# The products of p and V as four 32-column tiles of the TensorE array

## The chip, the cores and the metric

The kernel runs on one core of one Trainium2 chip. The metric is device time in microseconds (us); lower is better. Times of single instructions are in nanoseconds (ns). PE is TensorE's matmul, PEld its weight load, ACT is ScalarE, DVE is VectorE, POOL is GpSimd, SP is SyncE, which issues most DMAs. L1172 is line 1172 of the kernel before.

## What is computed

Three results are put together: a recurrent attention with memory over 64 segments of 32 tokens, a gated feed-forward block over all 2048 tokens, and a gate that mixes the two. All inputs are bf16; the width is 640, there are 32 heads of 192, the memory has 8 rows.

```python
for s in range(n_seg):                       # 64 segments, one after the other
    h = concatenate([mem, x[:, 32*s:32*s+32]], axis=1)      # 8 + 32 rows
    q, k, v = (einsum('btd,dhe->bhte', h, W) for W in (Wq, Wk, Wv))
    scores = where(mask, einsum('bhqe,bhke->bhqk', q, k) * scale, -1e9)
    p = softmax(scores, axis=-1)
    o = einsum('bhqk,bhke->bhqe', p, v)      # the product of p and V
    o = einsum('bhte,hed->btd', o, Wo)
    mem = o[:, :8]                           # the next segment needs it
    outs.append(o[:, 8:])
a = concatenate(outs, axis=1)
b = (gelu(x @ w_gate) * (x @ w_up)) @ w_down
out = g * a + (1 - g) * b                    # g = sigmoid((x * gate_w).sum(-1))
```

The memory makes the segments a chain: segment s+1 can't begin before the first rows of segment s are there.

## The kernel before, in words

The feed-forward block comes first (`ffn_gu`, `ffn_down`, the first 190 us or so of the execution). Then come the 64 segments, in `segment`. Weights of the attention don't all fit in the on-chip memory: most pieces stay there, and 17 slots (14 of 384 KB for Wq, Wk and Wv, 3 of 480 KB for Wo) hold two pieces by turns and are loaded anew in each segment by SP (`load_piece`, L597), as soon as the matmuls that read the old piece are done.

The order of the work within a segment is written out by hand in the list `PROG` (L504). Its entries are: `g` (the projections of a group of Q, K, V, one of five slices of the contraction at a time, L1039, and L226 where the weights in the array are kept), `tq` and `tk` (transposes of Q and K rows on DVE, L1073), `sc` (scores, L1080 to L1093), `ex` (softmax on DVE and ACT), `pt` (p is transposed on TensorE, L1139 and L1144, and ACT copies it out of PSUM, L1157), `pv` (the product of p and V, `pv_oct`), `wo` (the output projection, L1201, in the last octet L1224), and `lf` and `vb` (projections for rows of later segments, L882 and L1012). A segment has four octets of 8 heads (4 pairs of heads); `pv` stands in the list once for each. The engines' queues are filled in this order, and each engine works its queue off in order. Semaphore waits are put in by `_Sched`: an operation waits for the last writer of what it reads and for the readers of what it writes. If a PE operation has several waits, some may be moved onto the last instructions of the operation before it.

TensorE can be split by columns. A matmul with `tile_position=(0, 32*j)` and 32 columns of weights uses a quarter of the array and writes the PSUM partitions 32j to 32j+31; four of those, for j = 0 to 3, are issued one after another and run side by side. The projections, the transposes of p and the output projection are all of that kind. The scores use two halves of the array (40 columns of weights at column 0 or 64).

In `pv_oct`, for one octet: V is in `v_sb` (128 partitions: the 32 rows of the segment for each of 4 pairs), the part of V for the 8 memory rows of 4 segments is in `vl_sb`, and the transposed p is in `PTm` and `PTl` (index i: first or second head of a pair). The output has 384 columns of V, in three chunks c of 128; in chunk c the columns 64i to 64i+63 belong to head i. `half(c, i)` makes two matmuls for the 64 columns: one against `PTm[:, i]`, 160 columns moving (L1172), and one against `PTl[:, i]`, 64 columns moving, which adds to some of those results (L1174). Each matmul brings a weight load of its own. They are issued in the order of c, first the two of L1172 and then the two of L1174. So an octet has 12 matmuls and 12 weight loads. In every fourth segment (s % 4 == 0) the first of these stand in an operation of their own, named PV, which doesn't wait for `vl_sb`; the rest (PVa) does. After that ACT (L1183), and in the last octet also DVE (L1188), copies the result out of PSUM, and `wo` uses it.

Of the kernel before, what the change touches and what calls it, by code (L numbers as in the profile page):

```python
# [231 lines left out]
def _build(nc, A_x, A_mem0, A_Wq, A_Wk, A_Wv, A_Wo, seg_len, w_gate, w_up, w_down,  # L232
# [34 lines left out]
    S_ = _Sched(nc)  # L267
# [27 lines left out]
    NVB, NUB = 2, 2  # L295
# [35 lines left out]
    ps = nc.alloc_psum_tensor("ps", [128, 8, 512], F32)  # L331
# [3 lines left out]
    o = wsA_base - wsB_total  # L335
# [6 lines left out]
    o = wsA_base  # L342
# [4 lines left out]
    o = ffn_base  # L347
# [10 lines left out]
    def sreg(o, nbytes, plo=0, phi=128):  # L358
        return Rg("sb", o, o + nbytes, plo, phi)
# [35 lines left out]
    r_v = [sreg(wsB_off["v"] + b * 768, 768) for b in range(NVB)]  # L395
# [8 lines left out]
    PTm = PT[:, 0:PTW].rearrange("p (i t r) -> p i t r", t=4, r=R)  # L404
    PTl = PT[:, PTW:PTW + 128].rearrange("p (i t r) -> p i t r", t=4, r=16)
    r_PT = sreg(wsB_off["PT"], 2 * (PTW + 128))
# [23 lines left out]
    o = ffn_base - sum(fp_sz.values())  # L430
# [48 lines left out]
    r_ps = [Rg("ps", b, b + 1) for b in range(8)]  # L479
# [45 lines left out]
    def octet(s, i):  # L525
        return i if s % 2 == 0 else NOCT - 1 - i
# [35 lines left out]
    o = 0  # L562
# [71 lines left out]
    def load_residents(cls, pick=lambda key: True):  # L634
        for key in first:
# [7 lines left out]
           reads=[r_ident], writes=[r_ident])  # L643
    def asel(ap, reg, pattern, base, cm, fill):
# [12 lines left out]
           reads=[r_elw], writes=[r_elw])  # L657
# [19 lines left out]
    for h in range(NH):  # L677
        for w_, sb_, rw_, nm in ((w_gate, wg_sb, r_wg, "wg"), (w_up, wu_sb, r_wu, "wu")):
            S_.add("sp", lambda e, h=h, w_=w_, sb_=sb_: e.dma_start(
                sb_[h], w_.rearrange("(p k) f -> p k f", p=128)[:, :, FH * h:FH * (h + 1)]),  # L680
                writes=[rw_[h]], dma_sem="%s%d" % (nm, h))
# [228 lines left out]
    for n, (g, o) in enumerate(units):  # L910
# [7 lines left out]
        if g == 0:  # L918
            S_.add("pool", lambda e, o=o, b=b: e.tensor_copy(out=stg[:, o], in_=lst[b][:, 0]), reads=[r_lst[b]], writes=[r_stg[o]],
                   name="stg s0 o%d" % o)  # L920
# [69 lines left out]
    def misc_bank(s, group=9):  # L990
        tick[0] += 1
        ok = [b for b in (0, 1, 2, 3) + ((LB,) if s % 4 in (1, 2) or s % 4 == 3 and group < 3 else ()) + ((OB,) if group < 2 else ()) if b not in bk_of.values() and b not in lb.values()]
        b = min(ok, key=lambda b: misc[b])
        misc[b] = tick[0]
        return b

    def apx(ap, dims):
        return bass.AP(ap.tensor, ap.offset, [list(ap.ap[0])] + [list(d) for d in dims])
# [161 lines left out]
    def pv_oct(s, o):  # L1160
        A = misc_bank(s)
        B = misc_bank(s) if o in USPLIT else A
        oc = octet(s, o)
        v, vl, u = v_sb[o % NVB], vl_sb[oc], uT[o % NUB]
        ru = r_uTp[o % NUB]
        W = 4 * R

        def half(c, i):
            full = ps[64 * i:64 * i + 64, B if c == 2 else A, W * c:W * c + W]
            part = full.rearrange("p (t r) -> p t r", r=R)[:, :, XA:R]  # L1170
            e0 = 128 * c + 64 * i
            return [lambda e: e.matmul(full, v[:, e0:e0 + 64], PTm[:, i], start=True, stop=False,  # L1172
                                       tile_position=(0, 64 * i), skip_group_check=True),
                    lambda e: e.matmul(part, vl[:, e0:e0 + 64], PTl[:, i], start=False, stop=True,  # L1174
                                       tile_position=(0, 64 * i), skip_group_check=True)]

        fns = [x for c in range(3) for y in zip(half(c, 0), half(c, 1)) for x in y]
        if s % 4 == 0:
            S_.add("pe", fns[:2], reads=[r_v[o % NVB], r_PT], writes=[r_ps[A]], name="PV s%d o%d" % (s, o))
            del fns[:2]  # L1180
        S_.add("pe", fns, reads=[r_v[o % NVB], r_vl[oc], r_PT], writes=[r_ps[A]] + ([r_ps[B]] if B != A else []), name="PVa s%d o%d" % (s, o))
        na = 2 if o in USPLIT else 3
        S_.add("act", lambda e: e.activation(  # L1183
            out=apx(u[:, 0, 0, :], [[R, na], [3 * R, 4], [1, R]]),
            in_=ps[:, A, 0:na * W].rearrange("p (c t r) -> p c t r", t=4, r=R), func=ACTF.Copy),
            reads=[r_ps[A]], writes=[ru[0]] if na == 2 else ru, name="uT evac s%d o%d" % (s, o))
        if na == 2:
            S_.add("dve", lambda e: e.tensor_copy(out=u[:, :, 2, :], in_=ps[:, B, 2 * W:3 * W].rearrange("p (t r) -> p t r", r=R)),  # L1188
                   reads=[r_ps[B]], writes=[ru[1]], name="uT mid s%d o%d" % (s, o))
        q = s % 4  # L1190
        S_.add("pool", lambda e: e.tensor_copy(  # L1191
            out=uTl[:, 12 * oc:12 * oc + 12, M * q:M * q + M].rearrange("p (t c) i -> p t c i", c=3), in_=u[:, :, :, L:R]),
            reads=[r_uT[o % NUB]], writes=[r_uTl[oc]], name="uTl s%d o%d" % (s, o))
# [71 lines left out]
    def segment(s):  # L1265
# [3 lines left out]
        for n, item in enumerate(PROG):  # L1269
# [25 lines left out]
            elif kind == "pt":  # L1295
                p_transp(s, i)
            elif kind == "pv":
                pv_oct(s, i)
            elif kind == "lf":
                if i == q and unit(s, item[2]):  # L1300
                    if item[3] == 0:
                        for m in range(2):
                            lb[item[2], m] = misc_bank(s)
                    for m in range(2):
                        LBK[m] = lb[item[2], m]
                    left_mm(*unit(s, item[2]), item[3], unit_piece)
            elif kind == "vb":
                if q == 3 and g + 1 < NG:
                    if i == 0:
                        lb["v"] = misc_bank(s)  # L1310
                    vl_mm(s + 1, i)
            elif kind == "le":
                if i == q and unit(s, item[2]):
                    if n > n_wo:
                        post.append(item[2:])
                    else:
                        left_evac(s, *item[2:])
            else:
                held = wo_part(s, item)
                if i == 2 and item[2] == 0 and q == 0 and g > 0:  # L1320
                    outl_store(g - 1)
                if q == 3 and item != items[-1]:
                    wo_left(s, held)
# [116 lines left out]
```

## Time and profile before

| | |
|---|---|
| Median of 3 runs | 1802.42 us (1795.88 to 1802.75) |
| Span of the profiled execution, first to last instruction | 1783.4 us |
| Mean granted TensorE clock | 0.998 |
| PE busy | 1629.5 us, 91% |
| Chain that ended last | PE 69%, DMA 13%, DVE 8%, ACT 6%, issue 4% |
| Data moved by DMA | 524.33 MB, 294 GB/s over the span |
| L1172: 1536 matmuls, mean of one | 243 ns |
| L1174: 1536 matmuls, mean of one | 194 ns |
| Weight loads of L1172 and L1174, mean of one | 109 and 112 ns |

The profile gives of the profiled execution its span; the runs' times also hold what lies around the span, and a time of the profiled execution with that is not shown. Busy time counts a time once in which several matmuls of an engine overlap, and a matmul's mean is its length from start to modelled end. "issue" stands for time in which an engine waited for nothing that the profile shows. A table of windows has, for each stretch, its length, the busy time of PE, PEld, DVE, ACT and POOL with the number of instructions in brackets, the granted clock, the DMA engines' share (by packets that start in the window, so it can pass 1) and GB/s.

### The profile page before, as it was taken

The numbers are of one execution on the slowest core, as the hardware profiler recorded it, in microseconds if no ns is written. First come the engines' busy times: TensorE is split into PE (matmuls) and PEld (weight loads), VectorE is DVE, ScalarE is ACT, GpSimd is POOL, SyncE is SP. The second block draws the span as 40 slices with busy tenths as digits, with TensorE's granted clock in tenths as the row PEclk, the third lists the DMA queues.
The fourth block names the chain that finished last, engine by engine and source line by source line (L and its number), as shares of the span: only waits on it lengthen the run. The fifth ranks groups of instructions, "written<-read, shape, count | busy, mean of one in ns | idle before, by whom it ended". The sixth has DMA issues, their size and how long they took to land.

```text
span 1783.4 us, 80070 instructions
## 1 busy us (share of the span) xinstructions
PE 1629.5 (91%) x39162; PEld 817.9 (46%) x31501; DVE 957.7 (54%) x2932; ACT 793.8 (45%) x1835; POOL 319.8 (18%) x1099
## 2 busy tenths in 40 slices
PE   9999989899998999899899999899999989899987
PEld 4554444454444444454444444454444444454443
DVE  2223555555555655555565655555555655555554
ACT  3222444444444444444444444444444544444443
POOL 1100111111211111111111111111211111111211
PEclk9999999999999999999999999999999999999999
DMA  9815887888788887888788887888888887888786
GB/s 332 297 45 177 329 318 266 324 322 316 289 295 298 318 311 261 318 318 315 287 299 299 311 319 263 322 310 319 298 299 300 317 290 269 321 313 321 289 303 260
DMA packets 263390, 524.33 MB, mean 294 GB/s; under 512 B 97384, under 2 KB 116224, under 8 KB 263040
## 3 DMA queue, kind: packets, MB, share of 16 engines
q1 hardware_dynamic: 259912, 516.11, 79.5%
q8 instruction: 276, 4.52, 1.0%
q10 hardware_dynamic: 3128, 3.09, 0.5%
q14 instruction: 74, 0.61, 0.1%
HBM read 498.00 MB, written 21.11 MB: 291 GB/s over the span
## 4 chain that ended last, share of the span: by engine, by line
PE 69%; DMA 13%; DVE 8%; ACT 6%; issue 4%; SPq 0%; DVEq 0%; ACTq 0%
PE ps L1039 20%; PE ps L226 15%; PE ps L1201 8%; DMA arena<-in_A_Wv_dram 7%; PE ps L1172 3%; DMA left_qk_scratch<-arena 3%; PE ps L802 3%; PE ps L799 3%; PE ps L882 3%; DVE arena L889 3%; PE ps L1093 2%; PE ps L817 2%; ACT arena L887 2%; PE ps L1080 2%; PE ps L1088 2%
## 5 line engine op out<-in xcount | busy, mean ns | idle before, releaser
L1039 PE MATMUL ps<-arena 128*32 128x384 bf16 x9940 | 734.8, 328 | 58.5 <-DVE arena L1344 40.4
L226 PE MATMUL ps<-arena 128*32 128x384 bf16 x7680 | 584.4, 326 | 10.8 <-ACT arena L887 6.1
L1039 PEld LDWEIGHTS ps<-arena 128*32 128x32 bf16 x9940 | 254.0, 96 | 420.1 <-issue 244.4
L1073 DVE STREAM_TRANSPOSE arena<-arena 128x384 bf16<-128x384 bf16 x512 | 279.0, 564 | 227.0 <-ACT arena L1059 226.6
L1059 ACT ACTIVATE arena<-ps 128x384 bf16<-128x384 f32 x512 | 236.2, 489 | 176.3 <-PE ps L1039 164.4
L1201 PE MATMUL ps<-arena 128*32 128x320 bf16 x6144 | 297.0, 300 | 16.1 <-issue 15.5
L1201 PEld LDWEIGHTS ps<-arena 128*32 128x32 bf16 x6144 | 163.6, 97 | 75.7 <-issue 26.5
L1119 ACT ACTIVATE ps<-ps 104x160 f32<-104x160 f32 x256 | 74.3, 290 | 236.4 <-DVE ps L1109 236.4
L1107 DVE TENSOR_REDUCE arena<-ps 104x4 f32<-104x160 f32 x256 | 83.1, 325 | 176.0 <-PE ps L1093 175.7
L1157 ACT ACTIVATE arena<-ps 128x448 bf16<-128x448 f32 x192 | 104.8, 546 | 143.3 <-PE ps L1144 143.3
L1191 POOL COPY arena<-arena 128x96 bf16<-128x96 bf16 x256 | 68.4, 267 | 522.6 <-ACT arena L1183 419.3
L936 POOL COPY arena<-arena 128x96 bf16<-128x96 bf16 x256 | 70.0, 274 | 498.7 <-PE ps L1093 436.3
L1183 ACT ACTIVATE arena<-ps 128x480 bf16<-128x480 f32 (+1 forms) x256 | 138.1, 540 | 34.0 <-PE ps L1174 29.0
L1062 ACT ACTIVATE arena<-ps 128x384 bf16<-128x384 f32 x256 | 124.8, 488 | 52.7 <-PE ps L1039 52.4
L1172 PE MATMUL ps<-arena 128*64 128x160 bf16 x1536 | 122.1, 243 | 10.4 <-issue 3.4
L1172 PEld LDWEIGHTS ps<-arena 128*64 128x64 bf16 x1536 | 80.6, 109 | 97.9 <-ACT arena L1157 46.6
L882 PE MATMUL ps<-arena 128*32 128x384 bf16 x1280 | 111.1, 330 | 1.2 <-issue 1.2
L1174 PE MATMUL ps<-arena 128*64 128x64 bf16 x1536 | 105.1, 194 | 5.8 <-issue 5.8
L1121 DVE TENSOR_REDUCE arena<-ps 104x4 f32<-104x160 f32 x256 | 81.8, 320 | 51.6 <-ACT ps L1119 43.9
L889 DVE STREAM_TRANSPOSE arena<-arena 128x384 bf16<-128x384 bf16 x128 | 73.8, 577 | 57.4 <-ACT arena L887 52.6
L1224 PE MATMUL ps<-arena 128*32 128x160 bf16 x3072 | 77.1, 234 | 22.2 <-DMA arena<-in_A_Wo_dram 12.6
L887 ACT ACTIVATE arena<-ps 128x384 bf16<-128x384 f32 x128 | 62.4, 490 | 67.6 <-DVE arena L889 38.5
(84 smaller groups left out, 1816.7 us busy)
## 6 DMA issues: line engine op xcount, KB each, us to landing
arena<-in_A_Wk_dram SPq DMA_DIRECT2D x335, 384.0 KB, 7.7
arena<-in_A_Wv_dram SPq DMA_DIRECT2D x335, 384.0 KB, 9.4
arena<-in_A_Wq_dram SPq DMA_DIRECT2D x272, 384.0 KB, 5.6
arena<-in_A_Wo_dram SPq DMA_DIRECT2D x205, 480.0 KB, 7.4
left_qk_scratch<-arena SPq DMA_DIRECT2D x64, 192.0 KB, 2.6
arena<-left_qk_scratch SPq DMA_DIRECT2D x63, 192.0 KB, 7.8
ffn_b_scratch<-arena ACTq DMA_DIRECT2D x16, 160.0 KB, 3.7
arena<-ffn_b_scratch SPq DMA_DIRECT2D x64, 40.0 KB
```

What stands on the lines that cost most here:

```text
L226: return e.add_instruction(mybir.InstMatmult(name=nm, start_tensor_calc=like["start"], stop_tensor_calc=stop, tile_size=(128, 32), tile_po ...
L882: fns.append(lambda e, outp=outp, rhs=rhs, j=j: e.matmul(outp, lhs, rhs, start=(k == 0), stop=(k == KT - 1), tile_position=(0, 32 * j)))
L889: S_.add("dve", lambda e: e.transpose(out=dst[:, :, m].rearrange("p q c i -> p c q i"), in_=rowl.rearrange("p (c r) -> p c r", r=L)), read ...
L1039: fns.append(lambda e, outp=outp, rhs=rhs, j=j: e.matmul(outp, lhs, rhs, start=(k == 0), stop=(k == KT - 1), tile_position=(0, 32 * j)))
L1059: S_.add("act", lambda e, m=m, bk=bk: e.activation(out=rows_sb[m], in_=ps[:, bk, 0:384], func=ACTF.Copy), reads=[r_ps[bk]], writes=[r_rows ...
L1062: S_.add("act", lambda e, i=i, bk=bk: e.activation(out=v_sb[i % NVB].rearrange("p (c n) -> p c n", c=3), in_=ps[:, bk, 0:384].rearrange("p ...
L1073: S_.add("dve", lambda e: e.transpose(out=dst[:, :, 0:L], in_=rows_sb[m].rearrange("p (c r) -> p c r", r=L)), reads=[r_rows[m]], writes=[r ...
L1157: S_.add("act", lambda e: e.activation(out=PT, in_=ps[:, bank, 0:PTW + 128], func=ACTF.Copy), reads=[r_ps[bank]], writes=[r_PT], name="pT ...
L1172: return [lambda e: e.matmul(full, v[:, e0:e0 + 64], PTm[:, i], start=True, stop=False, tile_position=(0, 64 * i), skip_group_check=True), ...
L1174: lambda e: e.matmul(part, vl[:, e0:e0 + 64], PTl[:, i], start=False, stop=True, tile_position=(0, 64 * i), skip_group_check=True)]
L1183: S_.add("act", lambda e: e.activation(out=apx(u[:, 0, 0, :], [[R, na], [3 * R, 4], [1, R]]), in_=ps[:, A, 0:na * W].rearrange("p (c t r) ...
L1201: fns.append(lambda e, i=i, t=t, j=j, gv=gv: e.matmul(ps[32 * j:32 * j + 32, bank, 0:2 * DJ].rearrange("p (h n) -> p h n", h=2), lhs2[i], ...
```

## The change

`half(c, i)` becomes `tile(c, j)` with j = 0 to 3: 32 columns of V instead of 64, at the array's columns 32j, with the same moving data for j = 0 and 1 (`PTm[:, 0]`) and for j = 2 and 3 (`PTm[:, 1]`). An octet has 24 matmuls and 24 weight loads instead of 12 and 12, issued in the order of c, first the four against `PTm` and then the four against `PTl`. Each matmul has as many moving columns as before. The first part in every fourth segment has four matmuls instead of two. Nothing else is changed.

```diff
-        def half(c, i):
-            full = ps[64 * i:64 * i + 64, B if c == 2 else A, W * c:W * c + W]
+        def tile(c, j):
+            full = ps[32 * j:32 * j + 32, B if c == 2 else A, W * c:W * c + W]
             part = full.rearrange("p (t r) -> p t r", r=R)[:, :, XA:R]
-            e0 = 128 * c + 64 * i
-            return [lambda e: e.matmul(full, v[:, e0:e0 + 64], PTm[:, i], start=True, stop=False,
-                                       tile_position=(0, 64 * i), skip_group_check=True),
-                    lambda e: e.matmul(part, vl[:, e0:e0 + 64], PTl[:, i], start=False, stop=True,
-                                       tile_position=(0, 64 * i), skip_group_check=True)]
-
-        fns = [x for c in range(3) for y in zip(half(c, 0), half(c, 1)) for x in y]
+            e0 = 128 * c + 32 * j
+            return [lambda e: e.matmul(full, v[:, e0:e0 + 32], PTm[:, j // 2], start=True, stop=False,
+                                       tile_position=(0, 32 * j), skip_group_check=True),
+                    lambda e: e.matmul(part, vl[:, e0:e0 + 32], PTl[:, j // 2], start=False, stop=True,
+                                       tile_position=(0, 32 * j), skip_group_check=True)]
+
+        fns = [x for c in range(3) for y in zip(*[tile(c, j) for j in range(4)]) for x in y]
         if s % 4 == 0:
-            S_.add("pe", fns[:2], reads=[r_v[o % NVB], r_PT], writes=[r_ps[A]], name="PV s%d o%d" % (s, o))
-            del fns[:2]
+            S_.add("pe", fns[:4], reads=[r_v[o % NVB], r_PT], writes=[r_ps[A]], name="PV s%d o%d" % (s, o))
+            del fns[:4]
```

## The prediction, made before the result was known

> **What bounds the kernel now.** I read the page's busy shares first, then the PE's own waits, the PE timeline around a p·V product, and tables of short windows.
>
> ```profile
> PE 1629.5 (91%) x39162; PEld 817.9 (46%) x31501; DVE 957.7 (54%) x2932; ACT 793.8 (45%) x1835; POOL 319.8 (18%) x1099
> L1172 PE MATMUL ps<-arena 128*64 128x160 bf16 x1536 | 122.1, 243 | 10.4 <-issue 3.4
> L1174 PE MATMUL ps<-arena 128*64 128x64 bf16 x1536 | 105.1, 194 | 5.8 <-issue 5.8
> L1224 PE MATMUL ps<-arena 128*32 128x160 bf16 x3072 | 77.1, 234 | 22.2 <-DMA arena<-in_A_Wo_dram 12.6
> q8 instruction: 276, 4.52, 1.0%
> ```
>
> TensorE is nearly always busy, so its stream of instructions is what to look at. The mean of one matmul (243 ns) is latency, not cost: matmuls overlap, and the cost is the distance from start to start. That is in the timeline (columns: start, length, engine, line, operation):
>
> ```profile
> 991.11 0.34 PE L1039 MATMUL ps<-arena 128*32 128x384 bf16 x4
> 991.38 0.26 PE L1172 MATMUL ps<-arena 128*64 128x160 bf16 x2
> 991.47 0.20 PE L1174 MATMUL ps<-arena 128*64 128x64 bf16 x2
> 991.50 0.24 PE L1172 MATMUL ps<-arena 128*64 128x160 bf16 x2
> 991.57 0.20 PE L1174 MATMUL ps<-arena 128*64 128x64 bf16 x2
> 991.60 0.24 PE L1172 MATMUL ps<-arena 128*64 128x160 bf16 x2
> 991.67 0.20 PE L1174 MATMUL ps<-arena 128*64 128x64 bf16 x2
> 991.80 0.67 PE L1039 MATMUL ps<-arena 128*32 128x384 bf16 x12
> ...
> 998.33 0.58 PE L1201 MATMUL ps<-arena 128*32 128x320 bf16 x11
> 999.86 0.31 PE L1201 MATMUL ps<-arena 128*32 128x320 bf16 x1 [0.94 <-issue]
> ```
>
> One octet's p·V stands between two 32-column groups. Groups of 384 columns follow each other every 162.5 ns; into the 64-column pair it takes 256 ns (93 lost), and from the last pair to the next 32-column group 123 ns, where inside p·V the same pair takes 29 (93 lost). So each change of tile width leaves the array empty for 93 ns. The last two lines show something else: a stall in the middle of one product, where the PE waits for no engine and no DMA. The PE's waits put down to "issue" add up:
>
> ```profile
> PE ps L1201 <- issue: 15.5, 23, 1.7
> PE ps L1174 <- issue: 5.8, 8, 1.1
> PE ps L1039 <- issue: 4.1, 7, 1.0
> ```
>
> In the trace's records I find 67 such stalls after 200 us, 45.6 us in all (counted from where the moving columns end). Numbering the PE's records (weight loads and matmuls together), practically each stall ends at a record whose number is the same modulo 256, about 1.4 us after one 16 KB packet of the instruction queue has ended. Windows between such places show the count:
>
> ```profile
> 569.30:575.50 6.20, 5.10 (x128) 3.02 (x128) 2.71 (x10) 1.97 (x5) 1.13 (x4) 1.00 0.66 256
> 575.52:580.93 5.41, 5.41 (x149) 2.60 (x107) 2.25 (x7) 1.38 (x4) 0.94 (x4) 1.00 0.38 106
> 993.65:999.85 6.20, 5.19 (x132) 3.16 (x124) 2.24 (x9) 1.88 (x4) 0.27 (x1) 1.00 0.97 370
> ...
> 1216.00:1220.00 4.00, 3.60 (x88) 1.74 (x68) 2.61 (x8) 2.44 (x7) 0.80 (x3) 1.00 1.03 402
> 1228.00:1230.45 2.45, 0.73 (x32) 0.32 (x20) 1.59 (x5) 0.57 (x2) 0.82 (x2) 1.00 0.12 34
> ```
>
> The first counts are PE and PEld: 128+128, 149+107, 132+124, each 256 instructions, one packet of 16 KB (276 packets for 70,663 instructions). The packet for the next 256 starts only after the previous 256 have begun. Where the DMA engines are idle it starts about 1 us later, takes 1.04 us, and can be used 1.36 us after that: 3.5 us. From 3 to 19 us into each segment the weight swaps fill the DMA engines (share 1.03, 402 GB/s), and the packet starts 3 to 4 us later. **By time since the segment's start**, next page usable / page taken, means in us: begun at 4.5 to 9: 4.7 to 5.2 / 5.5 to 5.6; at 9 to 18: 5.5 to 6.1 / 5.7 to 6.2; after 18: 4.6 falling to 3.4 / 5.6 to 6.8. So in the middle of a segment the PE already runs at the pace at which its instructions arrive, within 0.1 to 0.3 us a page.
>
> **The change, part by part.** *Removed: two changes of tile width per octet.* 178 of the 256 octets enter with no wait (93 ns each, 16.6 us); the others begin 53 ns after an ACT evacuation ends, as any waiting instruction does, so their drain is hidden and nothing is won there. 252 leave straight into other work: 23.4 us. What is late next is the instruction supply (below).
>
> *The product itself.* Now it is 327 ns without the exit: starts at 0, 93, 121, 194, 222, 295, then 29. Afterwards it is three times a group of four with 160 columns plus one with 64. The first is in the trace: L1224 has this form, and its groups follow every 69 ns, members 3 to 4 ns apart, a weight load for each. The second is not. Bounds: 29 ns, the pace of today's pairs (the same 64 columns stream), and 40 ns, the pace of L1139's group of four with 80 columns; less than 29 is excluded since the columns stay. I take 35, between two near rows: 3 x (69+35) = 312, 15 ns won, 3.8 us in all (bounds 0 to 8). PE time saved: 16.6+23.4+3.8 = 44 us, 0.17 us an octet.
>
> *Added: instructions.* 12 more matmuls and, as each L1172 and L1174 matmul has a weight load now, 12 more loads: 24 per octet, 6144 in all, 24 pages more. A price for a page boundary from both sides: nothing, if the PE takes longer over 256 instructions than the next page needs; the whole pace, 5.7 us/256 = 22 ns an instruction, where it is already bound. Octets 0, 1 and 2 of a segment start at 8 to 9, 11 to 13 and 14.5 to 16.5 us, in the bound stretch. After the change a page with p·V in it holds about 4.6 us of work there (5.4 x 174/198, less the saved gaps), under the 5.5 to 6.1 that the next page needs. So the rows say the full pace: 3 x 24 x 22 ns = 1.6 us per segment, and the saved drains there only turn into longer stalls. The slack that is there now is the mean 0.32 us a page over the 2.35 pages of 4.5 to 18 us, 0.75; one page's slack can't serve another, so I take 0.6. The fourth octet, at 19.5 to 22 us, lies where pages come in 3.5 to 4.6 us: its 24 instructions cost nothing, and it wins 0.17.
>
> *What hides some of it.* PE waits that end with a weight landing come to 17.7 us for Wo, 16.0 for Wv, 6.1 for Wk. Those of Wo stand behind all of this in the segment, with their landing set by a full DMA queue, so they take in delay one for one: 0.28 us a segment; of the others, most of which lie within the bound pages, I count a quarter, 0.09. That no such wait is left costs 0.37 us a segment.
>
> *Waits.* None is added. In every fourth segment the first part (which doesn't wait for vl) has four matmuls instead of two; the octet's ACT evacuation waits for the last matmul as before, and that starts 0 to 33 ns earlier after the first. SP's weight loads wait for matmuls; those late in the segment issue later with the PE, behind a full queue.
>
> *Sum.* 1.60-0.60-0.17-0.37 = 0.46 us a segment; 64 segments: +29 us on the span of 1783.4. The runs shown (median 1802.42) lie 12 to 19 us above the span; added to the median: **1831 us**.
>
> **The rivals.**
>
> 1. *The drains decide: faster.* The 44 us come off the PE, which is busy 91%, and instructions are no limit. For: the 93 ns are exact, and PE leads the chain. Against: the 67 stalls at 256. About half the segments end on a weight landing and give theirs back: -22 us, 1780. It decides if the next page can be had within 4.6 us in the middle of a segment instead of 5.5 to 6.1. The Trainium skill, "Runtime: NRT & Kernel Launch", section "Instruction fetch mechanics", has the same 16 KiB blocks of 256 instructions but calls the cost of crossing one "mostly hidden"; by that rule this rival is the result. The trace disagrees, with 45.6 us of stalls at these crossings. Chance 0.15.
> 2. *The weight landings set the end: the same.* DMA at 400 GB/s for 17 of 25 us, then Wo. If all 0.64 us of landing waits take in delay, and the slack is 0.75, 1.60-0.75-0.17-0.64 = 0.04: +3 us, 1805. Against: many segments have no such wait. Chance 0.17.
> 3. *It doesn't do what it says:* groups of four run as two pairs. Then a product takes twice the pairs' pace, 6 x (69+29) = 588 instead of 312 ns, +71 us of PE time, less 40 of drains: +31, 1833, from another cause. Against it is L1224. A rule points this way: the Trainium skill, "TensorEngine Tiling (Array Packing)", section "Instruction Overhead", charges each matmul about 60 cycles, which more and smaller matmuls would pay; L1224's 48 starts within 0.78 us, 16.5 ns each, show no such charge. Chance 0.05.
>
> My forecast has 0.63. All from over 1811 up is slower by over 0.5% (about what a measurement of this kernel can tell from no change): 0.63+0.05; same 0.17; faster 0.15.
>
> **Range.** Low: rival 2 and the better part of rival 1, 1792. High: slack of 0.4 us, no landing that hides anything, 1.60-0.40-0.17 = 1.03 us a segment, +66: 1868. The forecast's own range is 1812 to 1868.
>
> **What would show it.** Right: p·V's first matmul 163 ns behind a 384-column group and the next group 30 to 40 ns behind the last; groups of four 69 and 29 to 40 ns apart; 42,234 matmuls, 34,573 weight loads, 300 instruction packets; PE idle by "issue" over 80 us, the stalls still 256 records apart; fewer waits on Wo. Wrong: stalls no more than now (rival 1), segments of the same length with longer waits for weights (rival 2), or starts of pairs 69 ns apart within a group (rival 3).

## The result and the profile after

The changed kernel is slower: median 1879.43 us (1876.1 to 1884.01, 4 runs) against 1799.58 (1795.88 to 1802.75, 4 runs) for the kernel before, ratio 1.0436 [1.0403, 1.0468], some 80 us more. The prediction had the direction and the mechanism, +29 us, and a range that ended at 1868; the measured time lies outside it.

In all runs from here on the time is 1.7 to 1.9 us above the span. So the profiled execution of before, with its span of 1783.4 us, was itself one of about 1785 us, some 14 below the median; the two profiles lie 91 us apart where the medians lie 80 apart. Accounts made from the two traces are too large by about 11 us for that reason.

The page of the changed kernel (busy shares, instruction queue, the chain that ended last, the two groups of p·V):

```profile
PE 1612.4 (86%) x42253; PEld 838.3 (45%) x34573; DVE 958.3 (51%) x2932; ACT 792.3 (42%) x1835; POOL 319.0 (17%) x1099
q8 instruction: 300, 4.92, 1.0%
PE 68%; issue 10%; DVE 10%; DMA 6%; ACT 6%; SPq 0%; DVEq 0%; ACTq 0%
L1172 PE MATMUL ps<-arena 128*32 128x160 bf16 x3072 | 122.8, 235 | 18.4 <-issue 12.6
L1174 PE MATMUL ps<-arena 128*32 128x64 bf16 x3072 | 110.4, 193 | 7.9 <-issue 7.7
```

TensorE does *less* busy work than before (1612.4 against 1629.5 us), and yet the span is longer: its share fell from 91 to 86%. Instructions and packets are those forecast (34,573 loads, 300 packets; 42,253 matmul records against 42,234; the trace of before lacks 19, having 39,162 where light_before with the same matmuls has 39,181). In the chain, "issue" rose from 4 to 10% while DMA fell from 13 to 6%.

One octet's p·V in the timeline of after (start, length, engine, line, operation, tile, count):

```profile
902.42 0.67 PE L1039 MATMUL ps<-arena 128*32 128x384 bf16 x12
902.92 0.24 PE L1172 MATMUL ps<-arena 128*32 128x160 bf16 x4
902.99 0.20 PE L1174 MATMUL ps<-arena 128*32 128x64 bf16 x4
903.02 0.24 PE L1172 MATMUL ps<-arena 128*32 128x160 bf16 x4
903.09 0.20 PE L1174 MATMUL ps<-arena 128*32 128x64 bf16 x4
903.12 0.24 PE L1172 MATMUL ps<-arena 128*32 128x160 bf16 x4
903.19 0.20 PE L1174 MATMUL ps<-arena 128*32 128x64 bf16 x4
903.22 0.34 PE L1039 MATMUL ps<-arena 128*32 128x384 bf16 x4
```

Groups of four start 0.07 and 0.03 us apart, the next 384-column group 0.03 us behind the last. First start to next product is 0.30 us; before, from 991.38 to 991.80, it was 0.42, and the entry had another 93 ns. So the product itself became about 0.2 us quicker, as forecast. The time went elsewhere; these are the PE's waits in after (waiting engine and line, what ended the wait: total us, times, longest us; L1344 writes the memory rows for the next segment, L1073 transposes rows of Q and K):

```profile
PE ps L1201 <- issue: 51.3, 40, 2.3
PE ps L1039 <- DVE arena L1344: 50.2, 48, 2.0
PE ps L1039 <- issue: 27.9, 30, 1.9
PE ps L1172 <- issue: 12.6, 12, 1.6
PE ps L1174 <- issue: 7.7, 9, 1.7
PE ps L1224 <- DMA arena<-in_A_Wo_dram: 0.5, 1, 0.5
PEld ps L1088 <- DVE arena L1073: 14.2, 61, 0.5
```

The same rows of before, as far as they weren't shown:

```profile
PE ps L1039 <- DVE arena L1344: 40.4, 48, 1.8
PE ps L1224 <- DMA arena<-in_A_Wo_dram: 12.6, 22, 0.9
PEld ps L1088 <- DVE arena L1073: 1.3, 6, 0.2
```

All of the PE's "issue" rows together grew from 36.5 to 142.6 us. The stalls still come every 256 records. Two windows of after that lie between such places, PE and PEld counts adding to 257 and 255 (a window's edge takes one more or less):

```profile
1071.35:1077.54 6.19, 4.69 (x133) 2.57 (x124) 2.42 (x8) 2.40 (x6) 0.55 (x2) 1.00 1.04 382
1077.56:1083.80 6.24, 4.75 (x146) 2.22 (x109) 3.06 (x11) 2.27 (x6) 1.80 (x6) 1.00 0.37 102
```

Each page is worked off in about 4.7 us of PE time and takes 6.2. Counted in the trace's records (idle PE from the end of the moving columns, in the 64 segments):

| idle PE time, us | before | after | difference |
|---|---|---|---|
| stalls at page boundaries | 56 | 171.5 | +115 |
| waits on weights landing (Wo, Wv, Wk) | 38.1 | 14.3 | -24 |
| gaps under 130 ns, among them the drains (the 93 ns at a change of tile width) | 127.7 | 88.2 | -40 |
| waits on DVE (L1344 44.9 to 58.3, L1073 5.5 to 16.0, L1125 10.7 to 14.0, L1188 6.3 to 9.0) | 67.4 | 97.3 | +30 |

That sums to +81 of the 89.6 us by which the segments grew; the rest lies in small rows. Before, nearly all stalls ended 12 to 24 us into a segment, 50 us in all; after, they fill 9 to 24 us with about 38 us in each 3-us bin from 12 on.

### The profile page after: what moved, and what is told of

Read it like the earlier page. It is cut to its first block, busy times and chain, and to the rows that moved or that the text cites. A ratio compares the mean times of both kernels' runs of the same rounds, so it can differ in the third digit from the quotient of the medians.

```text
span 1874.4 us, 86233 instructions
## 1 busy us (share of the span) xinstructions
PE 1612.4 (86%) x42253; PEld 838.3 (45%) x34573; DVE 958.3 (51%) x2932; ACT 792.3 (42%) x1835; POOL 319.0 (17%) x1099
## 4 chain that ended last, share of the span: by engine, by line
PE 68%; issue 10%; DVE 10%; DMA 6%; ACT 6%; SPq 0%; DVEq 0%; ACTq 0%
PE ps L1039 19%; PE ps L226 14%; PE ps L1201 8%; DMA arena<-in_A_Wk_dram 3%; PE ps L799 3%; PE ps L802 3%; PE ps L1224 3%; PE ps L1172 3%; PE ps L1093 3%; PE ps L882 2%; PE ps L817 2%; DMA arena<-in_A_Wv_dram 2%; PE ps L1088 2%; PE ps L1080 2%; DVE arena L889 1%
## 5 line engine op out<-in xcount | busy, mean ns | idle before, releaser
L1039 PE MATMUL ps<-arena 128*32 128x384 bf16 x9940 | 753.1, 330 | 89.1 <-DVE arena L1344 50.2
L226 PE MATMUL ps<-arena 128*32 128x384 bf16 x7680 | 601.0, 328 | 15.6 <-ACT arena L887 5.8
L1039 PEld LDWEIGHTS ps<-arena 128*32 128x32 bf16 x9940 | 266.0, 97 | 443.8 <-issue 276.9
L1073 DVE STREAM_TRANSPOSE arena<-arena 128x384 bf16<-128x384 bf16 x512 | 278.9, 564 | 270.0 <-ACT arena L1059 269.6
L1201 PE MATMUL ps<-arena 128*32 128x320 bf16 x6144 | 309.0, 301 | 52.6 <-issue 51.3
L1201 PEld LDWEIGHTS ps<-arena 128*32 128x32 bf16 x6144 | 176.6, 97 | 109.0 <-issue 64.8
L1172 PE MATMUL ps<-arena 128*32 128x160 bf16 x3072 | 122.8, 235 | 18.4 <-issue 12.6
L882 PE MATMUL ps<-arena 128*32 128x384 bf16 x1280 | 119.1, 330 | 13.5 <-issue 13.4
L1174 PE MATMUL ps<-arena 128*32 128x64 bf16 x3072 | 110.4, 193 | 7.9 <-issue 7.7
L1172 PEld LDWEIGHTS ps<-arena 128*32 128x32 bf16 x3072 | 84.1, 96 | 69.7 <-ACT arena L1062 21.7
L1109 DVE TENSOR_TENSOR ps<-ps,arena 104x160 f32<-104x160 f32 x256 | 85.1, 332 | 8.8
```

The lines of the kernel that those rows point to most:

```text
L226: return e.add_instruction(mybir.InstMatmult(name=nm, start_tensor_calc=like["start"], stop_tensor_calc=stop, tile_size=(128, 32), tile_po ...
L882: fns.append(lambda e, outp=outp, rhs=rhs, j=j: e.matmul(outp, lhs, rhs, start=(k == 0), stop=(k == KT - 1), tile_position=(0, 32 * j)))
L1039: fns.append(lambda e, outp=outp, rhs=rhs, j=j: e.matmul(outp, lhs, rhs, start=(k == 0), stop=(k == KT - 1), tile_position=(0, 32 * j)))
L1073: S_.add("dve", lambda e: e.transpose(out=dst[:, :, 0:L], in_=rows_sb[m].rearrange("p (c r) -> p c r", r=L)), reads=[r_rows[m]], writes=[r ...
L1172: return [lambda e: e.matmul(full, v[:, e0:e0 + 32], PTm[:, j // 2], start=True, stop=False, tile_position=(0, 32 * j), skip_group_check=T ...
L1174: lambda e: e.matmul(part, vl[:, e0:e0 + 32], PTl[:, j // 2], start=False, stop=True, tile_position=(0, 32 * j), skip_group_check=True)]
```

## The experiments

**Theory A:** the number of PE instructions decides, because while the weight swaps fill the DMA queues TensorE waits for its pages. **Theory B**, the rival: the matmuls of the new form themselves cost the time. Further experiments take the terms of A's sum apart. Each time stands against runs of the kernel before on the same chip. "At equal count" means as many PE instructions as before.

**1. Fewer weight loads (after_kept).** Weights are loaded only for the first of the three products; the other 20 matmuls of an octet run with the weights that are there. 28 instructions an octet instead of 48 (before: 24), with the same 24 matmuls.

```diff
+            if c:
+                first = lambda e: _kept_free(e, full, ...)        # matmul without a weight load
+            else:
+                first = lambda e: e.matmul(full, v[:, e0:e0 + 32], PTm[:, j // 2], ...)
```

> The four tiles as in the changed kernel, with the same matmuls and the same moving columns, but weights are loaded only for the first group of four of an octet; the other 20 matmuls use what is in the array, so most of the product is computed with wrong weights. An octet has 28 PE instructions, against 24 before the change and 48 after it. Theory A (the pace at which instructions arrive): 4 pages of 256 more than before instead of 24, and the drains gone: 1775 to 1815 us. Rival B (four 32-column tiles cost time by themselves): near the changed kernel's 1879, 1860 to 1890. If it were the weight loads' own time in the array and not their number, the time would fall too, but groups of four would stand closer together than after the change.

Measured: 1821.44 us, before 1794.12, ratio 1.0138 [1.011, 1.0166]. That is 6 us above A's range and far below B's: 54 of the 80 us go with 20 loads an octet. B is out. That the loads cost by their own time in the array, and not by their number, is out too: in this trace groups of four follow each other in 69 ns (160 columns) and 28 ns (64 columns), with a load or without, as in after.

**2. More instructions, nothing else (before_tiny).** The kernel before with 12 matmuls of one moving column (and 12 loads) more in each octet.

```diff
+        tiny = [lambda e, i=n % 2: e.matmul(ps[64*i:64*i+64, A, 0:1], v[:, 64*i:64*i+64], PTm[:, i, 0, 0:1],
+                                            start=True, stop=True, tile_position=(0, 64*i), ...) for n in range(12)]
+        S_.add("pe", tiny, reads=[r_v[o % NVB], r_PT], writes=[r_ps[A]], ...)
```

> The kernel before, with 12 more matmuls of one moving column in front of each octet's product, each with its weight load: 24 more PE instructions an octet, as in the change, but two tiles of 64 columns as before. Their results are overwritten by the product. Theory A: stalls as many as after the change, and the drains stay: +80 to +130 us, 1880 to 1930. Rival B: only the array time of 6 pairs, at most 25 ns a pair by the pairs of L1088, 38 us in all: 1800 to 1838.

Measured: 1886.59 us, before 1794.12, ratio 1.0518 [1.0477, 1.0559]. The same number of instructions as the change costs as much or a little more, though there is hardly any arithmetic in them. Page and PE waits of this run:

```profile
q8 instruction: 300, 4.92, 1.0%
PE ps L1204 <- issue: 42.4, 43, 1.7
PE ps L1039 <- issue: 20.0, 23, 1.9
```

The rows are those of after (L1204 is its L1201): the stall falls on whatever product stands at the 256th record, not on p·V.

**3. The new form at equal count (after_kept_all).** As 1, with no weight load in p·V at all: 24 instructions an octet, all in 32-column tiles.

```diff
-            if c:
-                first = lambda e: _kept_free(e, full, ...)
-            else:
-                first = lambda e: e.matmul(full, v[:, e0:e0 + 32], PTm[:, j // 2], ...)
+            first = lambda e: _kept_free(e, full, ...)
```

> The four tiles with no weight loads at all: all 24 matmuls of an octet use what earlier work left in the array (the product is computed with wrong weights). An octet has 24 PE instructions, as before the change, in the new form. It tells what the form does at an equal count. Theory A: within 1% of the kernel before, 1780 to 1812, and below the run with 28 instructions (1821) by 4 pages, 5 to 25 us. Rival B (something in the form itself costs): still 1815 or more.

Measured: 1794.28 us (10 runs), before 1797.22, ratio 0.9991 [0.9972, 1.0011].

```profile
PE 1606.8 (90%) x42253; PEld 730.2 (41%) x28429; DVE 958.6 (53%) x2932; ACT 793.7 (44%) x1835; POOL 321.9 (18%) x1099
q8 instruction: 276, 4.52, 1.0%
PE ps L1209 <- issue: 22.8, 27, 1.9
```

L1209 is L1201 here. As many packets as before (276), as many matmuls as after (42,253), no drains in p·V, and the time of before. So the new form alone costs nothing, and the drains it saves bring nothing: the first product still stands 163 ns behind a 384-column group and the next one 28 ns behind the last, but the PE's "issue" rows come to 51.6 us instead of 36.5. From 24 to 28 instructions an octet (experiments 3 and 1) the ratio rises by 0.0147, 26 us for 1024 instructions, 26 ns each (22 with experiment 4 in place of 1): full price from the first one on.

**4. Is the place in the page what counts? (after_kept_shift).** Experiment 1 with 64 matmuls of one column once, ahead of the feed-forward block, which move all page boundaries by half a page.

```diff
+    S_.add("pe", [lambda e: e.matmul(ps[:, 4, 0:1], ident, ident[:, 0:1], ...) for _ in range(64)], ...)
```

> The run with weights loaded only for the first group of an octet (28 instructions, 1821 us), with 64 tiny matmuls and their weight loads put once at the very start, where the PE waits for its first data. They shift all later page boundaries by half a page and cost nothing else. In that kernel four segments hold 17.0 pages, so every boundary comes at the same place in each round of four segments. Theory A with that: the place of the boundaries counts, and the time moves by 8 us or more, likely down, 1795 to 1813. If the 27 us come from the four weight loads an octet alone: unchanged, 1816 to 1827.

Measured: 1817.78 us, before 1796.87, ratio 1.0117 [1.0084, 1.015], the same as experiment 1 within the intervals. The 25 us were no accident of where the boundaries fell. What the added time consists of does depend on it: from experiment 3 to 1 the PE's "issue" rows grow by 6 us only (51.6 to 57.9) and its waits for Wo and Wk by 10 (23.4 to 33.8); with the shift "issue" grows by 22 (to 73.6) and those waits fall by 11 (to 12.7).

**5. The swaps made light (light_before, light_after, light_tiny).** The weight swaps move an eighth of their data; the rest of a slot keeps the other piece. The first is otherwise the kernel before, the second the changed one, the third the kernel of experiment 2.

```diff
+        dst, src = piece_view(key, res_off[key]), piece_src(key)
+        if name[:4] == "swap":
+            dst, src = (dst[:, 0:1, 0:240], src[:, 0:1, 0:240]) if key[0] == 3 else (dst[:, 0:192], src[:, 0:192])
-        S_.add("sp", lambda e: e.dma_start(piece_view(key, res_off[key]), piece_src(key)), ...)
+        S_.add("sp", lambda e: e.dma_start(dst, src), ...)
```

> The kernel before, where each swap of a weight piece moves an eighth of the piece (the rest of the slot keeps the other piece, so the result is wrong). The DMA engines are then far from full. Theory A: the next 256 instructions can be had 3.5 us after the last 256 have begun, in the whole segment; the PE idle time by issue falls from about 37 us to under 10, no wait for a weight landing is left: 1700 to 1750 us. Rival C (the PE itself is the bound and stalls are of no weight): 1750 to 1795.

> The changed kernel with the same light swaps. Theory A: no stalls for instructions, so only the drains are left of the change: 20 to 45 us below the kernel before with light swaps. Rival B (the four tiles cost time by themselves): 40 us or more above it.

> The kernel before with light swaps (an eighth of each swapped piece is moved, so the result is wrong) and the 12 tiny matmuls with their weight loads an octet. With full swaps those 24 instructions cost 92 us. Theory A (each page waits for a packet behind the weight swaps): with empty DMA engines only their array time is left: 0 to 38 us above light swaps alone, 1726 to 1764, without stalls at page boundaries. If a boundary has a price of its own, whatever the DMA engines do: 60 us or more above, 1785 or more.

Measured: 1725.54 us for light_before (ratio to before 0.9607 [0.9583, 0.963]), 1709.6 for light_after (0.952 [0.9498, 0.9542]), 1754.2 for light_tiny (0.9767 [0.9738, 0.9796]). Page and waits of light_before (all lines of the code lie 3 further down, so L1091 is L1088):

```profile
DMA  9824621222222221222222222222222222222221
PE 1602.5 (93%) x39181; PEld 812.6 (47%) x31501; DVE 955.5 (55%) x2932; ACT 792.4 (46%) x1835; POOL 319.4 (19%) x1099
PEld ps L1091 <- DVE arena L1076: 0.2, 1, 0.2
PE ps L1142 <- DVE arena L1129: 8.9, 18, 0.5
```

And of light_after:

```profile
PE 1574.9 (92%) x42253; PEld 810.3 (47%) x34573; DVE 955.8 (56%) x2932; ACT 791.8 (46%) x1835; POOL 319.5 (19%) x1099
PEld ps L1091 <- DVE arena L1076: 16.5, 82, 0.2
PE ps L1142 <- DVE arena L1129: 16.4, 32, 0.8
PE ps L1042 <- issue: 1.3, 1, 1.3
```

With the DMA engines at two tenths the PE has no "issue" row in light_before, and one of 1.3 us in light_after, at 300 packets of instructions. Now the change is *faster*, by 16 us, with a direction opposite to that of the full kernel. The 12 tiny matmuls still cost 28.7 us, 9 ns for each matmul with its load, and there is no "issue" row of the PE in that run either: 24 more page boundaries, and no stall at any. So a boundary by itself has no price, and of the 93 us of experiment 2 at most 29 are array time. The Trainium skill, "Runtime: NRT & Kernel Launch", section "Instruction fetch mechanics", calls the cost of crossing a block "mostly hidden". That holds in this pair, and does not hold beside full weight queues (142.6 us of "issue" in after).

The 16 us fall short of the expected 20 to 45 and of the 44 us of saved drains. The two waits shown say where the rest went: the scores wait for the transposed rows of Q and K (L1076) 16.5 us instead of 0.2, the transposes of p for the softmax (L1129) 16.4 instead of 8.9. An engine that comes 93 ns earlier to a result that isn't ready has won nothing.

**6. One octet at a time (tiles_o3, tiles_o012, tiles_o0).** The new form only in the fourth octet, only in the first three, or only in the first; the others as before.

```diff
+        if o == 3:                                        # o < 3, o == 0 in the other two
+            fns = [x for c in range(3) for y in zip(*[tile(c, j) for j in range(4)]) for x in y]
+        else:
+            fns = [x for c in range(3) for y in zip(half(c, 0), half(c, 1)) for x in y]
```

> Four tiles in the fourth octet of a segment alone, two tiles in the other three. The prediction had it that there the 24 instructions cost nothing and 0.17 us is won: 64 x 0.17 = 11 us faster, about 1785. The new reading is that the page which holds this octet was begun before 18 us, while the DMA engines were full, so the instructions cost there as elsewhere: 10 to 35 us slower, 1805 to 1830.

> Four tiles in the first three octets, two in the fourth. If the prediction's step on the fourth octet was right, all of the change's +80 us and 11 more is here: 1880 or more. By the new reading the octets share it: 1840 to 1870.

> Four tiles in the first octet of a segment alone. Its 24 instructions come at 8 to 9 us. The prediction's slack of 0.6 us a segment would take in all of 24 x 22 ns = 0.53 us: no change, 1787 to 1802. If slack in one page can't serve the next, so that the instructions cost their pace: +15 to +35 us, 1810 to 1832.

| | us | before | ratio | difference, us |
|---|---|---|---|---|
| tiles_o3 | 1808.63 | 1797.22 | 1.0061 [1.0041, 1.0081] | +11 |
| tiles_o012 | 1887.01 | 1797.22 | 1.0491 [1.0468, 1.0515] | +88 |
| tiles_o0 | 1824.38 | 1796.87 | 1.0142 [1.0104, 1.0181] | +26 |
| all four (the change) | 1879.43 | 1799.58 | 1.0436 [1.0403, 1.0468] | +79 |

The first octet alone costs 26 us for its 1536 instructions, 17 ns each, where a slack of 0.6 us a segment would have swallowed all 24 (0.53 us). The fourth alone costs 11 us, against the 11 us that the prediction's step would have won; beside the other three it does win about 10 (1.0436 against 1.0491), as that step says, though the two intervals touch. The reading made after the first four runs (experiments 1 and 2, light_before and light_after) gave tiles_o012 at least 17 us too little. The terms don't simply add.

**7. Drains taken out and put in at other places (pv_by_sc, one_mask).** The first takes `sc` and `pv` next to each other in `PROG`, so that four changes of tile width a segment go (24 us of PE time) with the same instructions. The second writes the mask of the scores with one matmul of 128 columns instead of two of 40: 512 instructions fewer, one change of width more.

```diff
-            ("pt", 1), ("sc", 2), ("lf", 1, 0, 2), ("g", 4, 4), ("pv", 1),
+            ("pt", 1), ("lf", 1, 0, 2), ("g", 4, 4), ("sc", 2), ("pv", 1),
-            ("g", 5, 4), ("pv", 2), ("wo", 1, 1), ("tk", 3),
+            ("g", 5, 4), ("wo", 1, 1), ("pv", 2), ("tk", 3),
```

```diff
-        for gp in (0, 64):
-            fns.append(lambda e, gp=gp: e.matmul(ps[gp:gp + R, bank, SC:512]..., ident[:, 0:R], maskm..., tile_position=(0, gp), ...))
+        fns.append(lambda e: e.matmul(ps[0:128, bank, SC:512]..., ident, maskm..., ...))
```

> The kernel before with another order and no instruction more: the second octet's product stands directly behind the scores of the third, and the third's product directly before the scores of the fourth, so that work with tiles over 32 columns stands together and four of the changes of width in a segment are gone, 4 x 93 ns x 64 = 24 us of PE time. If drained time is worth its length: 1765 to 1778. By the new reading (the pace of instructions and the waits of the score chain take it): within 8 us of the kernel before, 1786 to 1802.

> The kernel before with fewer instructions: the mask of an octet's scores is put into PSUM by one matmul of 128 columns (with the mask's rows a second time in partitions 64 to 103) instead of two of 40 columns, one matmul and one weight load an octet less, 512 in all, with one more change of tile width. By the price per instruction seen here (16 to 26 ns): 8 to 13 us faster, 1784 to 1789. If the further change of width counts at its 93 ns: 24 us more, 1805 to 1815.

pv_by_sc: 1796.99 us (12 runs), before 1797.22, ratio 0.9996 [0.9978, 1.0014]: the drains that it saves are worth nothing here. It isn't a clean test of them, since the new order brings a wait of the scores that before has no row for:

```profile
PE ps L1088 <- DVE arena L1073: 13.3, 43, 0.3
```

one_mask: 1828.79 us, before 1797.19, ratio 1.0185 [1.0159, 1.0211]; both expectations were missed. Its timeline at one product of scores:

```profile
887.13 0.24 PE L1080 MATMUL ps<-arena 128*128 128x160 bf16 x1
887.31 0.27 PE L1087 MATMUL ps<-arena 128*40 128x40 bf16 x8
887.51 0.27 PE L1092 MATMUL ps<-arena 64*40 64x40 bf16 x8
```

From the mask to the first scores it takes 0.18 us, where before the two mask matmuls were followed after 0.08 or 0.09: in the trace's records 173 against 80 ns, 93 more. The Trainium skill, "TensorEngine Tiling (Array Packing)", section "Key Properties", says that a change of the tiling mode drains the array; this place agrees and gives the price. 256 of them are 24 us. So a drain that is *added* ahead of the scores seems to cost its length, while those *removed* around p·V brought nothing. That leaves some 8 us and the value of 512 instructions fewer unexplained; the stalls at boundaries grew from 56 to 83 us in this run, and why isn't settled.

**8. Instructions where the DMA engines are idle (before_pad, before_pad_shift).** 8 matmuls of one column and 8 loads at the end of each segment in the kernel before; the second also with the shift of experiment 4.

```diff
+        S_.add("pe", [lambda e, j=i % 4: e.matmul(ps[32*j:32*j+32, OB, 0:1], ident[:, 0:32], ident[:, 0:1],
+                                                  tile_position=(0, 32*j), ...) for i in range(8)], ...)
```

> The kernel before with 8 tiny matmuls and their weight loads at the end of each segment, where the PE waits for the memory rows: 16 instructions a segment, which also makes 17.0 pages in four segments instead of 16.7. Nothing else waits for them. At the full pace of 22 ns an instruction: +23 us, 1820. If the end of a segment, with the DMA engines empty, takes them at no cost and the place of the boundaries counts: anywhere from 1775 to 1820, and not the same as with the shift.

> The same with all page boundaries half a page earlier by 64 tiny matmuls at the start. If the place of the boundaries counts: 8 us or more away from the run without the shift. If not: within 5 us of it.

Measured: 1800.44 us (10 runs), ratio 1.0028 [1.0007, 1.0049], +5 us; shifted 1807.37, ratio 1.0049 [1.003, 1.0067]. The 16 instructions a segment that cost 26 us between experiments 3 and 1 cost 5 here, a fifth. Whether the shift changes anything can't be told: the medians are 7 us apart, between the two expectations, and the intervals of the ratios overlap. No version of these was faster than the kernel before with the full weight traffic and the whole computation.

## Why the prediction was right in direction and wrong in size

- **The mechanism is shown.** It was that instructions, not array time, limit TensorE in the middle of a segment. The "issue" rows grew fourfold, every 256 records; 12 one-column matmuls an octet cost what the change costs, or a little more (2); the same form at equal count costs nothing (3); with light swaps the change is faster (5). Rivals 1 and 3 are out: the drains didn't decide, and groups of four run as four. Rival 2 is out by the time and by its sign: the waits for weights became shorter, not longer. (Rival 3's sum was off by 4 us: against the 327 ns of today's product its 588 ns are +67 us, so +27, not +31.)
- **"Full pace, 22 ns an instruction": right.** 26 ns (3 against 1), 17 ns (first octet alone). Over all 6144 instructions the change cost 80 us, 13 ns each, since part of it is hidden and the fourth octet adds none.
- **"That no such wait is left costs 0.37 us a segment" (weight landings): right.** These waits fell by 24 us, 0.37 for each of 64; the close agreement is partly luck, since the waits that were to be counted at a quarter (Wv, Wk) changed unevenly.
- **"The fourth octet costs nothing and wins 0.17": right in company** (-10 us, forecast -11), wrong alone (+11). It may be that it can win only when the first three octets have already made the segment late; no run shows that directly.
- **"The slack that is there now: I take 0.6": the step that failed.** It was worth 38 us of the sum and is worth about nothing. The 0.32 us by which a page is longer than the next page needs is a mean, and most of it lies in the page begun 4.5 to 9 us into the segment. The 24 instructions of the first octet should have fitted into it and cost 26 us. At 22 ns each they are 34 us, and tiles_o0's waits for Wo and Wv fell by 9 (21.9 to 12.7), so nothing is left for slack to have taken in. Four instructions an octet cost 22 to 26 ns each, wherever the boundaries lie (1, 3, 4). In after, pages within 0.25 us of the moment when the next one could be used rose from 105 of 262 to 165 of 285.
- **The sum without it:** 1.60-0.17-0.37 = 1.06 us a segment, +68 us, against 80 measured; for the first three octets alone 1.23, +79, against 88 [84, 93]. About 10 us are left. They would fit a term that the prediction put at nothing ("None is added"), the waits on other engines (+30 us in the table): 14 us of it (L1073 and L1125) are of the kind that the light pair shows, where PE's saved drains turn partly into waiting for DVE's transposes and for the softmax and 16 of 44 us were left. Another 13 us are the wait for the memory rows (L1344), which fell in the light pair; why it grew isn't shown. How the 10 us divide between these and longer stalls isn't settled.
- **The range** ended where slack was 0.4 and no landing hid anything. The bound of slack should have been nothing; with the fourth octet at nothing too, that reaches 1.60 us a segment, 102 us, and the time lies inside. (The stalls by themselves grew by 115 us, from a profile of before that was some 11 us short.) The bound came from a mean over pages, without asking where in the segment the slack lay.

## What to carry to other kernels

Where the DMA queues are as full as here, count the instructions of the busiest engine as well as its array time: look in its timeline for stalls in the middle of a product, 256 records apart, put down to "issue", and take every added instruction at the full pace of a page (6.2 us for 256 here, 24 ns each), with no credit for a mean slack. A gap that is removed from an engine is worth something only if the next operand is there earlier too; ask for each one what the next wait is. Less weight traffic beside the busy stretch helped (1725.54 us with light swaps, which leave out seven eighths of the swapped weights), fewer drains did not.

## What the runs showed of the hardware

- A page of 256 PE instructions is usable about 3.5 us after the previous one has begun where the DMA engines are idle, 5.5 to 6.1 us where weight swaps fill them (trace of before). TensorE worked one off in 4.7 us of busy time (the two windows of after, which took 6.2); the difference is the stall.
- A change of tile width costs 93 ns each way between 32 and 64 columns (before), and as much from 128 to 40 (one_mask). Groups of four within the 32-column form have none; in after they follow each other in 69 ns (160 columns) and 28 ns (64 columns; pairs of 64-column tiles take 29).
- An added PE instruction cost 17 to 26 ns in the stretch with full queues (tiles_o0, experiments 1 and 3), and 5 to 9 ns at the end of a segment (before_pad and before_pad_shift, 5 and 9 us by their ratios for 1024).
